# Maxima over partitions by two matmuls, x ahead of the weights, and a wider pace of phase one

## The chip, the core and the metric

The kernel runs on one core of a Trainium2 chip. A core has a matrix engine (TensorE, PE in the profile; PEld is its weight load), a vector engine (VectorE, DVE), an activation engine (ScalarE, ACT), a general engine (GpSimd, POOL) and a sync engine that issues most of the transfers (SyncE, SP). The engines share a 128-partition memory (SBUF), PE writes to banks of PSUM, and each engine takes its instructions strictly in its program's order. The metric is the device time of one execution in microseconds (us), and lower is better.

## The reference

Two branches work on x, 8192 rows of 448 values:

```
xn = layernorm(x)
s  = irfft2( soft( W2 . relu( W1 . rfft2(xn) + b1 ) + b2 ) )      # complex, 4 blocks of 112
g  = silu( ( gelu(xn @ w_gate) * (xn @ w_up) ) @ w_down )         # 448 -> 1792 -> 448
out = x + s * g
```

`soft` moves every value towards zero by 0.01 and cuts at zero. The transform runs over the 8192 rows. The result has to be FP32-accurate, so each FP32 value is split into two or three FP16 values, and a product becomes three FP16 matmuls. For the split, the weights are scaled by a power of two that is taken from the largest magnitude of a block.

## The kernel before

x is worked on in 16 chunks of 512 rows (each 4 tiles of 128 rows). Two streams of work share the engines.

The feed-forward stream (`ffn`, `chunk`, `unit`, `down`) goes over all chunks twice: pass 0 with the first 8 of 14 weight blocks of 128 columns, pass 1 with the other 6. That makes 32 feed-forward chunks, numbered 0 to 31 here. Each chunk first multiplies x by the gate and up weights (tiles `xta`, `xtb` by `wt`, into the banks `bx` and `by`), forms the gated product `h` on ACT, DVE and POOL, and then multiplies by the down weights (`h` by `dw`, into `bd`). Chunk 0 is special (`begin`, `token`, `plain`): it normalises and transposes its x itself, on PE, and starts while the weights are still being prepared.

The transform stream has three phases. Phase one (`chunk1`, once per x chunk) normalises x (`stats`, `norm`), makes the FP16 factors that the feed-forward stream reads later (stored to `xts` and read back transposed into `xta` and `xtb`), and does the first transform matmuls (`stage1`, `m` by `xs` into `bf`). Phase two (`zero`, then 32 groups in `group`) does the second transform stage, both complex layers and the way back. Phase three (`tiles3`) does the last inverse stage and writes the output.

The weights are prepared on the chip. `gu_block` finds the largest magnitude of one or two weight blocks: DVE reduces along the free dimension into `fm` and `fx`, and `largest` takes the maximum over the 128 partitions. From that come exponents (`fe`, `fh`, `fc`), and `gu_split` splits the block on ACT and DVE into `wt`. `gu_combs` loads the block again and forms sums and differences on POOL (`cb`), for a scheme that saves matmuls. `down_weights` does the same for the down weights (`dmx`, `dw`), `prep_mlp` for the weights of the transform's layers (`mst`, `ms`). `largest` is called 11 times: eight times for gate and up (five for chunk 0), twice for the down weights (once for chunk 0), once in `prep_mlp`. In the kernel before it is one POOL instruction, a collective over partitions:

```
G.partition_all_reduce(dst, src, channels=128, reduce_op=bass_isa.ReduceOp.max)
```

The order of the work is made by a small planner (`Pace`), not by hand. Every call of an engine goes through `Pace.issue` (so nearly all instructions carry line 167), which keeps a modelled clock for each engine with the costs in `Pace.cost`, and the coroutines of the kernel are continued in the order of these modelled times. The engines then run the instructions in that fixed order, each waiting on semaphores for what it needs. Two numbers set the pace of phase one: chunk c of phase one may start at the modelled time T1 + (c - 1) x DT. Phase two spreads its 32 groups evenly from its start to a fixed modelled time (END2, 1440), and phase three from there to END3 (1790). Memory for tiles is taken from rings with few buffers; four buffers (`wst`) hold raw weight blocks.

Of the kernel before, what the change touches and what calls it, by code (L numbers as in the profile page):

```python
# [22 lines left out]
CH = 4  # L23
# [12 lines left out]
EPS = 1e-5  # L36
# [8 lines left out]
class Pace:  # L45
# [96 lines left out]
    def cost(self, e, op, n, out, ins):  # L142
# [4 lines left out]
        if e == "ACT":  # L147
            return 0.17 + 0.00086 * n
        if e == "POOL":
            if op == "partition_all_reduce":  # L150
                return 4.0
            return 1.3 if n < 8 and op == "tensor_tensor_pow" else 0.2 + 0.0024 * n
        two = len([i for i in ins if i.free_size() == n and i.space != bass.MemoryType.PSUM]) > 1
        return 0.12 + (0.0014 if two else 0.00107) * n
# [136 lines left out]
def afno_geglu_kernel(ctx, tc, x, gu, wd, mlp, b1, b2, c_m, c_mt, c_small, out):  # L291
# [46 lines left out]
    fx = cp.tile([128, 2, NBK], F32, name="fx")  # L338
# [18 lines left out]
    def largest(dst, src):  # L357
        G.partition_all_reduce(dst, src, channels=128, reduce_op=bass_isa.ReduceOp.max)
# [17 lines left out]
    SX = ring(p1, [128, 4 * 480], F16, "sx", 2)  # L376
    YS = ring(p1, [128, 2, 2, D], F16, "ysb", 2)
# [16 lines left out]
    def load_x(c):  # L394
        x4 = EV["x4", c] = yield from X4.get()
        n2 = CH * (c % NG)
        for a in ((0, 2) if c == 0 else (0,)):
            m = 2 if c == 0 else CH
            Q.dma_start(x4[:, a:a + m, :], xv[:, n2 + a:n2 + a + m, :])
        if c == 0:  # L400
            Q.dma_start(ident, c_small[:, 0:128])
        yield
        done("xl", c)
# [7 lines left out]
    def stats(c, E, gap=True):  # L411

        x4 = EV["x4", c]
        st = yield from ST.get()
        s6, mv, rs = st[:, :, 0:6], st[:, :, 6:8], st[:, :, 8:12]
        for a in range(CH):
            V.bn_stats(s6[:, a, :], x4[:, a, :])
            V.bn_aggr(mv[:, a, :], s6[:, a, :])
            if gap:
                yield  # L420
        v, y, t, r = (rs[:, :, i] for i in range(4))
        E.tensor_scalar(v, mv[:, :, 1], EPS, None, op0=ALU.add)
        G.tensor_tensor(y, v, mhalf, op=ALU.pow)
# [5 lines left out]
        EV["st", c] = st  # L429
# [118 lines left out]
    def gu_block(b, to):  # L548
# [20 lines left out]
        V.tensor_scalar(mxa, mxa, 2.0 ** -30, None, op0=ALU.max)  # L569
# [4 lines left out]
        MX.put(mxa)  # L574
# [63 lines left out]
    def down_weights(p):  # L638
# [40 lines left out]
        largest(dmx[:, 14 + fp0:14 + fp0 + nf], dmx[:, fs])  # L679
        yield  # L680
# [884 lines left out]
```

## Time and profile before

| What | Value |
|---|---|
| median of 3 runs | 1992.36 us (1990.3 to 1993.31) |
| profiled execution | 1995.1 us, span 1993.3 us |
| PE busy in the span | 1827.8 us (92%), mean granted clock 0.976 |
| DVE, ACT, POOL busy | 1162.6 (58%), 976.5 (49%), 602.1 (30%) us |
| chain that ended last, by engine | PE 73%, DVE 6%, DMA 5%, issue 4%, POOL 4% |
| DMA | 288.10 MB, mean 145 GB/s |

The profile shows one execution. The tables by stretches give, for each stretch of the span in us, its length, the busy time and instruction count of each engine, the clock that PE was granted (1 is full), the share of time that the DMA engines were busy, and what they moved. In the timelines a row has its start and duration in us, engine, line, operation, output and inputs, shape, and a count of merged instructions; in brackets stands how long the engine had been idle before it, and what ended that. "issue" there means that nothing in the profile was waited for.

### The profile page before, as it was taken

The numbers are of one execution on the slowest core, as the hardware profiler recorded it, in microseconds if no ns is written. First come the engines' busy times: TensorE is split into PE (matmuls) and PEld (weight loads), VectorE is DVE, ScalarE is ACT, GpSimd is POOL, SyncE is SP. The second block draws the span as 40 slices with busy tenths as digits, with TensorE's granted clock in tenths as the row PEclk, the third lists the DMA queues.
The fourth block names the chain that finished last, engine by engine and source line by source line (L and its number), as shares of the span: only waits on it lengthen the run. The fifth ranks groups of instructions, "written<-read, shape, count | busy, mean of one in ns | idle before, by whom it ended". The sixth has DMA issues, their size and how long they took to land.

```text
span 1993.3 us, 36110 instructions
## 1 busy us (share of the span) xinstructions
PE 1827.8 (92%) x14665; PEld 1348.7 (68%) x14665; DVE 1162.6 (58%) x1777; ACT 976.5 (49%) x1675; POOL 602.1 (30%) x612
## 2 busy tenths in 40 slices
PE   0777798897899999999999999999999999999998
PEld 0336566565677678778778778777777677777666
DVE  3577487677676554455455445566665456555445
ACT  1356455555465456555456455555555333333333
POOL 0177365464354312122112112112121233332111
PEclk9988899999899999999999999999999999999999
DMA  3465664665556330422221354334342698877662
GB/s 135 144 197 149 177 198 143 199 207 166 170 168 174 90 103 11 109 61 71 66 82 45 113 172 111 87 97 108 85 108 71 199 335 272 275 228 215 173 179 91
DMA packets 326296, 288.10 MB, mean 145 GB/s; under 512 B 236560, under 2 KB 293520, under 8 KB 326128
## 3 DMA queue, kind: packets, MB, share of 16 engines
q1 hardware_dynamic: 325984, 285.06, 48.8%
q8 instruction: 115, 1.88, 0.4%
q10 hardware_dynamic: 144, 0.72, 0.1%
q14 instruction: 53, 0.43, 0.1%
HBM read 129.36 MB, written 105.58 MB: 118 GB/s over the span
## 4 chain that ended last, share of the span: by engine, by line
PE 73%; DVE 6%; DMA 5%; issue 4%; POOL 4%; ACT 2%; SPq 2%; POOLq 0%; DVEq 0%; ACTq 0%
PE bx L167 23%; PE bd L167 20%; PE by L167 16%; PE bf L167 14%; DMA xta<-xts 2%; SPq L167 2%; DMA pt<-prt 1%; DVE h L167 1%; POOL st L167 1%; POOL xs L167 1%; DMA mt<-c_mt 1%; POOL cb L167 1%; DVE x L167 1%; DVE u L167 1%; POOL v L167 0%
## 5 line engine op out<-in xcount | busy, mean ns | idle before, releaser
L167 PEld LDWEIGHTS <-wt 128*128 128x128 f16 x8622 | 848.1, 99 | 220.8 <-issue 66.9
L167 PE MATMUL bx<-xta,wt 128*128 128x256 f16 (+1 forms) x4086 | 522.9, 281 | 37.1 <-ACT u L167 25.7
L167 PE MATMUL bd<-dw,h 128*128 128x448 f16 x2688 | 536.7, 355 | 17.9 <-DVE dw L167 5.8
L167 PEld LDWEIGHTS <-h 128*128 128x128 f16 x2688 | 262.7, 98 | 258.7 <-issue 23.1
L167 PE MATMUL by<-xtb,wt 128*128 128x256 f16 x2160 | 264.9, 276 | 22.2 <-ACT u L167 22.2
L167 POOL TENSOR_TENSOR v<-v,u 128x512 f32<-128x512 f32 x108 | 147.7, 1368 | 432.9 <-ACT v L167 339.1
L167 ACT COPY v<-bx 128x512 f32<-128x512 f32 x216 | 126.1, 584 | 123.5 <-PE bx L167 122.7
L167 PE MATMUL by<-xta,wt 128*128 128x256 f16 x1296 | 161.1, 275 | 0.0
L167 DVE SCALAR_TENSOR_TENSOR gl<-v,fc,gl 128x512 f32<-128x512 f32 (+1 forms) x123 | 97.6, 803 | 106.0 <-ACT gl L167 86.0
L167 DVE TENSOR_TENSOR h<-u,h 128x512 f16<-128x512 f32 x116 | 117.6, 1014 | 55.0 <-ACT h L167 54.4
L167 POOL TENSOR_TENSOR o<-o,c 128x896 f32<-128x896 f32 (+2 forms) x33 | 69.3, 2099 | 249.6 <-DVE c L167 249.6
L167 PE MATMUL bx<-xtb,wt 128*128 128x256 f16 x1080 | 135.6, 273 | 0.1
L167 DVE TENSOR_TENSOR u<-by,u 128x512 f32<-128x512 f32 x108 | 74.2, 687 | 84.8 <-PE by L167 84.7
L167 POOL TENSOR_TENSOR o<-o,x 128x448 f32<-128x448 f32 x60 | 80.6, 1347 | 125.6 <-DVE o L167 107.6
L167 POOL TENSOR_TENSOR wn<-h,wn 112x512 f16<-112x512 f32 (+2 forms) x36 | 37.8, 1049 | 267.0 <-issue 190.5
L167 ACT ACTIVATE gl<-bx,fc 128x512 f32<-128x512 f32 (+1 forms) x123 | 76.4, 635 | 82.5 <-PE bx L167 81.9
L167 ACT ACTIVATE u<-u,fc 128x512 f32<-128x512 f32 (+1 forms) x123 | 80.5, 667 | 65.5 <-DVE u L167 65.3
L167 DVE SCALAR_TENSOR_TENSOR u<-v,fc,u 128x512 f32<-128x512 f32 (+1 forms) x123 | 102.0, 839 | 9.2 <-ACT u L167 3.2
L167 ACT COPY u<-by 128x512 f32<-128x512 f32 x108 | 63.1, 584 | 84.8 <-PE by L167 61.8
L167 PE MATMUL bf<-z,w1t 112*112 112x512 f16 (+2 forms) x432 | 96.8, 357 | 4.7 <-DVE z L167 4.3
L167 ACT COPY u<-bx 128x512 f32<-128x512 f32 x108 | 62.9, 583 | 72.8 <-PE bx L167 72.2
L167 DVE TENSOR_TENSOR h<-gl,h 128x512 f16<-128x512 f32 x108 | 82.3, 762 | 23.5 <-ACT h L167 23.2
(133 smaller groups left out, 2210.4 us busy)
## 6 DMA issues: line engine op xcount, KB each, us to landing
xts<-sx SPq DMA_DIRECT2D x32, 480.0 KB, 2.7
wst<-in_gu SPq DMA_DIRECT2D x21, 704.0 KB, 5.8
x<-in_x SPq DMA_DIRECT2D x32, 448.0 KB, 6.0
x<-in_x SPq DMA_DIRECT2D x16, 896.0 KB, 6.0
t<-ysb SPq DMA_DIRECT2D x64, 224.0 KB, 3.1
prt<-th SPq DMA_DIRECT2D x64, 224.0 KB, 2.0
pt<-prt SPq DMA_DIRECT2D x64, 224.0 KB, 3.3
u<-t SPq DMA_DIRECT2D x32, 448.0 KB, 4.7
```

Of the source, the lines that this page charges most:

```text
L167: return self.pace.issue(self.name, kind, out, ins, lambda: fn(out, *args, **kw))
```

## The change

Three things change, and the planner's costs with them.

`largest` leaves POOL. It now takes the maximum over partitions by two FP32 matmuls with an FP32 identity matrix (`identf`). The first has the data as its stationary operand and the identity as the moving one, so its output is the transposed data, with w columns of partition maxima now on w partitions and 128 values along the free dimension. DVE takes the maximum along these 128 values into a small tile (`mxr`). The second matmul has this value, repeated 128 times, as stationary operand, and the identity of size w as moving one: its output has the w maxima on all 128 partitions. DVE reads it from PSUM, with a floor of 2 to the -30 (or 0) applied in the same instruction.

The first chunk of x comes in four loads of one tile each, in the order 0, 2, 1, 3, all on SP and ahead of the first weight block, which moves from ACT's queue to SP's. The FP16 identity moves to ACT's queue. Chunk 0's statistics are taken in two halves, tiles 0 and 2 first, each with its own power on POOL. ACT's first table load for Gelu stands behind the issue of the loads.

Phase one's T1 goes from 68 to 72 and its DT from 31 to 40, so that its 16 chunks are planned over more of the feed-forward stream. The cost model gets other numbers for ACT, POOL and DVE; these have no part in the computation, but they move instructions everywhere.

```
-            return 0.17 + 0.00086 * n
+            return 0.19 + 0.00086 * n + (0.08 if op != "copy" and n > 128 else 0.0)
...
-    def largest(dst, src):
-        G.partition_all_reduce(dst, src, channels=128, reduce_op=bass_isa.ReduceOp.max)
+    def largest(dst, src, floor):
+
+        w = src.shape[-1]
+        b = yield from BF.get()
+        T.matmul(b[0:w, 0:128], src, identf, start=True, stop=True)
+        yield
+        r = yield from MX.get()
+        V.tensor_reduce(r[0:w, 0:1], b[0:w, 0:128], axis=AXIS.X, op=ALU.max)
+        yield
+        T.matmul(b[:, 128:128 + w], r[0:w].to_broadcast([w, 128]), identf[0:w, 0:w], start=True, stop=True)
+        MX.put(r)
+        yield
+        V.tensor_scalar(dst, b[:, 128:128 + w], floor, None, op0=ALU.max)
+        BF.put(b)
...
         if c == 0:
-            Q.dma_start(ident, c_small[:, 0:128])
+            S.dma_start(ident, c_small[:, 0:128])
+            for a in (0, 2, 1, 3):
+                Q.dma_start(x4[:, a, :], xv[:, n2 + a, :])
+                pace.then(lambda a=a: done("xl", 0, a))
+            return
...
-    T1, DT = 68.0, 31.0
+    T1, DT = 72.0, 40.0
...
-            (S if f == 0 and not again else Q).dma_start(t, gu[f])
+            Q.dma_start(t, gu[f])
...
-        mxa = yield from MX.get()
-        mc = yield from MX.get()
-        V.tensor_copy(mc, mx)
-        largest(mxa, mc)
-        MX.put(mc)
-        yield
+        yield
+        mxa = fx[:, :, NBK + b]
+        yield from largest(mxa, mx, 2.0 ** -30)
...
+        def half(q):
+            yield from stats(0, V, (q, q + 2))
+            for a in (q, q + 2):
                 norm(0, a)
-                tasks.append(pace.spawn(token(a, xs), pace.last))
+                tasks.append(pace.spawn(token(a, xss[a // 2]), pace.last))
                 yield
+
+        yield ev("xl", 0, 2)
+        V.tensor_copy(identf, ident)
+        yield from half(0)
+        yield from half(1)
```

Three places show how the instructions move. The first is POOL at the start of the program. Before (`mxa` is the maximum over partitions, `st` the statistics of chunk 0, `xs` its FP16 halves; an `ISA` row without operands prepares POOL for other instructions):

```order
L167 MEMSET mhalf 128x4
L167 ISA
L167 ISA mxa<-mxa 128x2
L167 ISA
L167 TENSOR_TENSOR st<-st,mhalf 128x4
L167 ISA
L167 ISA mxa<-mxa 128x2
L167 ISA
L167 TENSOR_TENSOR xs<-x_95,xs 128x448
```

and in the change:

```order
L172 MEMSET mhalf 128x4
L172 ISA
L172 TENSOR_TENSOR st<-st,mhalf 128x2
L172 TENSOR_TENSOR xs<-x_95,xs 128x448
L172 TENSOR_TENSOR st<-st,mhalf 128x2
L172 TENSOR_TENSOR xs<-x_95,xs 128x448
L172 TENSOR_TENSOR cb<-wst 128x256
```

The collectives and the `ISA` rows around them are gone, one `ISA` row is left ahead of the first power, and the power now comes twice, for two tiles each.

The second place is a maximum for a far weight block, in feed-forward chunk 3. Before, on POOL (`sf`, `sx` are factors of phase one, `v` a partial sum of the feed-forward stream):

```order
L167 TENSOR_TENSOR sf<-x_1951 128x256
L167 ISA
L167 ISA mxa<-mxa 128x2
L167 ISA
L167 TENSOR_TENSOR sf<-x_1951,sf 128x192
L167 TENSOR_TENSOR v_2603<-v_2603,u_2506 128x512
```

In the change it is on PE, amid the gate and up matmuls of that chunk; the second matmul of the pair follows 39 matmuls later, behind `by<-xta,wt_79`:

```order
L172 MATMUL by<-xtb,wt_77 128x256
L172 MATMUL bf<-identf,fx 2x128
L172 LDWEIGHTS wt_76
L172 MATMUL bx<-xta,wt_76 128x256
...
L172 MATMUL by<-xta,wt_79 128x256
L172 MATMUL bf<-identf,mxr 128x2
L172 LDWEIGHTS wt_76
L172 MATMUL bx<-xtb,wt_76 128x256
```

POOL has its factors and partial sums in a row now, and PE has two short matmuls more, the second of which needs DVE's reduction.

The third place is the start of phase two on SP: the load of `y` from the first transform stage. Before, the ninth transposed load `xta` stands ahead of it (for feed-forward chunk 9):

```order
L167 DMA xts<-xs 128x2x128
L167 DMA_TRANSPOSE xta<-xts 128x16x256
L167 DMA y<-t 128x896
L167 DMA_TRANSPOSE xtb<-xts 128x9x256
L167 DMA prt<-th 128x448 x4
```

In the change eleven of them do:

```order
L172 DMA xts<-xs 128x2x128
L172 DMA prt<-th 128x448
L172 DMA y<-t 128x896
L172 DMA_TRANSPOSE xta<-xts 128x16x256
L172 DMA_TRANSPOSE xtb<-xts 128x9x256
```

Phase two starts in feed-forward chunk 11 instead of chunk 8, and in both orders ends in chunk 22. In chunks 1 to 6 stand 108 matmuls of `stage1` instead of 135.

More of the change, by code (lines that the diff above doesn't have):

```diff
@@ L409, in load_m, with stats @@
         done("m", c)
[L411 removed]
+    def stats(c, E, tiles=range(CH)):
         x4 = EV["x4", c]
[L414 removed]
+        if ("st", c) not in EV:
+            EV["st", c] = yield from ST.get()
+        st = EV["st", c]
         s6, mv, rs = st[:, :, 0:6], st[:, :, 6:8], st[:, :, 8:12]
[L416 removed]
+        for a in tiles:
+            if c == 0:
+                yield ev("xl", 0, a)
             V.bn_stats(s6[:, a, :], x4[:, a, :])
             V.bn_aggr(mv[:, a, :], s6[:, a, :])
[L419 removed]
+            if c:
                 yield
[L421 to L423 removed]
+        sl = slice(tiles[0], tiles[-1] + 1, tiles[1] - tiles[0])
+        v, y, t, r = (rs[:, sl, i] for i in range(4))
+        E.tensor_scalar(v, mv[:, sl, 1], EPS, None, op0=ALU.add)
+        G.tensor_tensor(y, v, mhalf[:, 0:len(tiles)], op=ALU.pow)
         yield
@@ L754, in prep_mlp @@
         m = ms[:, 2:6]
-        largest(m, st)
-        yield
+        yield from largest(m, st, 0.0)
         e1, e2, eH, eO = (ms[:, i:i + 1] for i in (6, 7, 8, 9))
```

41 lines of the change are left out of this document (19 added, 22 removed).

## The prediction

> **What bounds the kernel now.** I read the stages first: the busy time of each engine in seven stretches that I cut at the ends of the feed-forward chunks (150.42 below is the first matmul of chunk 1; chunk 7 is 576.8 to 634.4).
>
> ```profile
> core 0: us, PE busy (x) PEld busy (x) DVE busy (x) ACT busy (x) POOL busy (x), PEclk, DMA share, GB/s
> 0.00:50.00 50.00, 4.41 (x24) 2.19 (x24) 18.16 (x49) 7.37 (x15) 4.81 (x11) 1.00 0.35 134
> 50.00:148.90 98.90, 74.71 (x327) 34.81 (x328) 67.02 (x120) 44.26 (x75) 43.67 (x64) 0.88 0.55 171
> 148.90:576.80 427.90, 363.01 (x2593) 260.85 (x2591) 301.84 (x504) 227.49 (x415) 215.87 (x277) 0.92 0.60 176
> 576.80:634.40 57.60, 57.17 (x434) 42.24 (x432) 44.50 (x70) 33.93 (x62) 29.78 (x38) 1.00 0.63 171
> 755.50:1572.00 816.50, 811.85 (x7343) 626.63 (x7341) 444.89 (x616) 449.58 (x735) 165.00 (x108) 1.00 0.32 89
> 1572.00:1993.30 421.30, 399.96 (x2980) 292.62 (x2978) 221.90 (x309) 152.86 (x259) 115.56 (x87) 0.99 0.75 225
> ```
>
> From 576.8 on PE is the bound: it is idle 0.4 us in chunk 7 and 4.7 in the 816.5 after 755.5. Before that it is not: 45.6 us idle in the first 50, and chunks 1 to 6 take 427.9 us. Chunk 7 has the same matmuls (24 of the transform per chunk, 135 in those six), so six such chunks would take 6 x 57.6 = 346 us: 82 us are lost, 64.9 as idle time (427.9 - 363.0) and 17 as slower matmuls (363 - 346; granted clock 0.92). So I asked what PE waits for, first in the head, on POOL's timeline.
>
> ```profile
> 10.46 0.37 POOL L167 PARTITION_ALL_REDUCE mxa<-mxa  x1 [9.64 <-DVE st L167]
> 19.88 1.06 POOL L167 TENSOR_TENSOR st<-st,mhalf 128x4 f32<-128x4 f32 x1 [9.05 <-issue]
> 26.89 0.73 POOL L167 PARTITION_ALL_REDUCE mxa<-mxa  x1 [5.95 <-issue]
> 34.55 1.02 POOL L167 TENSOR_TENSOR xs<-x,xs 128x448 f16<-128x448 f32 x1 [6.94 <-issue]
> 41.66 0.37 POOL L167 PARTITION_ALL_REDUCE mxa<-mxa  x1 [6.09 <-issue]
> 49.02 1.02 POOL L167 TENSOR_TENSOR xs<-x,xs 128x448 f16<-128x448 f32 x1 [7.00 <-issue]
> 51.84 7.21 PE L167 MATMUL bx<-xta,wt 128*128 128x256 f16 x44 [0.31 <-ACT xta L167]
> ```
>
> The collective itself is short (0.37). But each change between it and an ordinary instruction leaves POOL 5.95 to 9.05 us with nothing to wait for ("issue"), in both directions. The normalisation's power (19.88) and two halves of x (34.55, 49.02) are queued behind, and the first real matmul starts at 51.84. In chunks 1 to 6 the same pair stands at five places; here the second of them on the timeline of all engines, then PE's rows at the others.
>
> ```profile
> 306.24 0.37 POOL L167 PARTITION_ALL_REDUCE mxa<-mxa  x1 [6.81 <-DMA xts<-xs]
> 313.31 0.58 POOL L167 TENSOR_TENSOR sf<-x,sf 128x192 f32<-128x192 f32 x1 [6.70 <-issue]
> 313.92 0.35 ACT L167 CAST sx<-sf 128x192 f16<-128x192 f32 x1 [8.17 <-POOL sf L167]
> 314.81 1.44 PE L167 MATMUL bx<-xta,wt 128*128 128x256 f16 x6 [6.96 <-ACT u L167]
> ...
> 226.85 0.35 PE L167 MATMUL bf<-xs,m 128*128 128x448 f16 x1 [3.11 <-DVE ysb L167]
> 234.89 0.90 PE L167 MATMUL bf<-xs,m 128*128 128x448 f16 x2 [7.68 <-POOL xs L167]
> 397.54 2.29 PE L167 MATMUL by<-xtb,wt 128*128 128x256 f16 x10 [6.34 <-ACT u L167]
> 479.62 2.29 PE L167 MATMUL by<-xtb,wt 128*128 128x256 f16 x10 [7.00 <-ACT u L167]
> 544.01 2.29 PE L167 MATMUL by<-xtb,wt 128*128 128x256 f16 x10 [8.49 <-ACT u L167]
> ```
>
> PE names ACT, ACT's own row names POOL, and POOL waited for nothing: ACT's eviction copy stands behind a cast that needs POOL. That is how a 0.37 us operation on an engine busy 30% stops PE for 7.
>
> **The head, -28 us.** Removed are six collectives and the changes around them. The chain that is left runs through DVE, and the last thing chunk 0 needs of it is the last split of the down weights.
>
> ```profile
> 20.97:51.80 30.83, 5.84 (x32) 3.03 (x33) 12.03 (x31) 5.28 (x12) 3.14 (x4) 1.00 0.13 47
> 51.80:132.30 80.50, 56.71 (x238) 25.70 (x238) 58.05 (x105) 36.75 (x65) 33.81 (x45) 0.87 0.47 152
> 132.33 16.59 PE L167 MATMUL bd<-dw,h 128*128 128x448 f16 x80 [1.71 <-DVE dw L167]
> 150.42 1.47 PE L167 MATMUL bx<-xta,wt 128*128 128x256 f16 x12 [0.47 <-DMA xta<-xts]
> ```
>
> From the power's end (20.9) to that split (132.3) DVE works 70.1 of 111.3 us, 63%. In the changed order two statistics (0.8 each) and two reductions (1.2 each) come behind the power too: 74. One load of POOL's code is left ahead of the first power. Its price is not shown for that place; nearest is the 9.05 after the first collective, started at 0.8, so the power ends at 0.8 + 9.05 + 1.06 = 11 (below: x halves land earlier and nothing is loaded, about 7). The Trainium skill's page "GPSIMD Engine Reference", section Instruction dispatch, puts about 6 us on the first call of freshly loaded code; by it the power would end near 8 and the sum be 3 us better; POOL's rows here run from 5.95 to 9.05 and I stay with the nearest. At DVE 100% busy the last split ends at 11 + 74 = 85, at today's 63% at 129. I take 80%, in the middle: 104, 28 earlier than 132.3. Chunk 1 follows it by the same 18.1 us as now (150.42 - 132.3: the last 16.6 us of matmuls and the transposing load), since the load on SP stays behind the first partial sum's store. Bounds -47 and -3.
>
> ```profile
> 0.00:10.00 10.00, 0.00 (x0) 0.00 (x0) 3.09 (x8) 1.49 (x2) 0.29 (x5) 1.00 0.82 311
> 6.77 1.22 DVE L167 TENSOR_REDUCE fm<-wst 128x2 f32<-128x1024 f32 x1 [6.77 <-DMA wst<-in_gu]
> ```
>
> The first weight block now stands behind all of x, 0.9 MB, on SP's queue instead of beside it on ACT's: at 311 GB/s 3 us, so it lands near 10 instead of 6.8. The wait for the power, until 11, covers it, as it covers the earlier first half of x: nothing; with the power at 7 it would be the 3 us.
>
> **The five places in chunks 1 to 6, -50.** PE's idle rows: 7.68 + 6.96 + 6.34 + 7.00 + 8.49 + 3.11 = 39.6 us. The slow clock behind them is shared out by idle time: 17 x 39.6 / 64.9 = 10.4. Together 50.
>
> **The two matmuls in their place, +7.** No 128-column FP32 matmul is in the trace; the nearest is the one on the sums of absolute values.
>
> ```profile
> L167 PEld LDWEIGHTS bf<-ab,onesf x8: 188/190/192, 515.0 to 522.7; 112*128 112x128 f32 x8
> L167 PE MATMUL bf<-ab,onesf x8: 537/538/542, 515.1 to 523.1; 112*128 112x448 f32 x8
> ```
>
> Four calls gave eight rows, two passes each. With 128 of 448 columns a pass is 0.15 us beside a 0.19 load: 0.7 for the first matmul, some 0.5 for the second, 1.2 for a pair and 6 for the five on PE's path; in the head PE is idle anyway. Between the two PE may arrive before DVE's reduction; the order leaves it 10 to 40 matmuls of other work, so I add 1. Above: uncut passes (0.54 + 0.19, four to a pair) are 15 for five pairs. Below: nothing, if the loads overlap. The second change has a queue price: PE is in order, so what stands behind a waiting second matmul waits too.
>
> **The lower pace in chunks 1 to 6, -10.** What is left of the 82 is 32: the largest piece is POOL and DVE late for the transform of the next chunk.
>
> ```profile
> 184.51 0.53 PE L167 MATMUL bf<-xs,m 128*128 128x448 f16 x1 [7.32 <-ACT xs L167]
> 180.00:190.00 10.00, 3.43 (x14) 1.89 (x14) 8.39 (x10) 4.69 (x7) 9.04 (x12) 0.50 0.01 2
> ```
>
> By the order the six chunks now hold 108 transform matmuls instead of 135, a fifth less. But without the stalls the rest comes in less time: DVE's 302 us, less some 18 for the work moved out, over 427.9 - 76 = 352 is 81% instead of 71%; chunk 7 runs clean at 77% (44.5 of 57.6). So I give a third back. Bounds 0 and -32.
>
> **A denser second phase, +5.** The phase now starts two to three chunks later and ends at the same chunk (the 23rd): 12 chunks do what 14 did. Even with everything 1.2 times denser DVE goes from 54% (444.89 of 816.5) to 65%, below chunk 7's 77%. I double the idle time there, 4.7. Bounds 0 and +25, three chunks of today's mean loss in chunks 1 to 6 halved (82 / 6 = 14, 7 each, rounded up). The last 421 us hold the same chunks and the same third phase, and PE sets their pace: nothing.
>
> **Sum:** -28 - 50 + 7 - 10 + 5 = -76. The profiled run has a span of 1993.3 and a time of 1995.1, 1.8 around it; it becomes 1917 and 1919. It was 2.7 above the median of the three runs, 1992.36, which becomes 1916.
>
> **The rivals.** *DVE takes over.* It feeds every eviction; nearly 100% busy where POOL's data come late, it could give half of the head and of the five places back and all of the pace: -14 - 25 + 7 + 5 = -27, about 1965; a milder form, last split at 118 and 15 us lost again in the chunks, gives -14 - 35 + 7 + 5 = -37, 1955. For it: 81% on an engine in order. Against it: chunk 7. *The pace takes all the rest* and DVE runs full in the head: -47 - 50 - 32 + 2 = -127, 1865. Against it: the head needs ACT, DVE and PE in turn for each weight block. *The second phase cannot be squeezed* (slower than before).
>
> ```profile
> 739.52 0.88 PE L167 MATMUL bf<-sm,y 128*112 128x128 f16 x12 [1.07 <-DMA y<-t]
> 1572.37 12.44 DMA xta<-xts
> ```
>
> Its 32 groups run from 739.5 to about 1572, 26.0 us each, through single buffers. In the change I expect the first near 122 + 11 x 59 = 771 and the end at 1572 - 76 = 1496: 22.7 each. If the chain of a group has a floor at 26.0, the phase ends at 1603, 107 later, and the run takes 2023; it is slower than before from a floor of 22.7 + 76 / 32 = 25.1. Against it: PE's only idle time there is 4.7 us, so PE and not the chain sets today's 26.0. *The collective is not the cause* and the matmuls only add: POOL's code loads stay in some other form, 1992 + 7 = 1999 at most. The Trainium skill, "GPSIMD Engine Reference", Engine selection, assigns a reduction along partitions to GPSIMD; by that rule the change would be this case. POOL's rows around each collective speak against it: no run here shows that price without one.
>
> **How the numbers follow.** Forecast 0.57, DVE takes over 0.22, the pace takes all 0.14, no squeeze 0.04, not the cause 0.03. The single bounds would reach from 1862 (-47 - 50 - 32 and nothing added) to 1992 and beyond; 1872 to 1958 leaves out about half of the pace case and the worse half of the DVE case, under 2 in 10. About 0.2% (4 us) can be told from no change here: faster 0.93, same 0.03, slower 0.04.
>
> **What would show it.** Right: POOL without idle "issue" rows behind 12 us; the first matmul on xta at 23 to 32; chunk 1's first at 108 to 136; chunks 1 to 6 in 60 to 64 us each, with no PE idle row over 5; idle PE time under 15 us between chunk 11 and the third phase; FP32 matmul rows under 0.3 us. Wrong: rows of 6 us and more on POOL beside the power; DVE at 95% over whole chunks with PE waiting for h, ysb or u; PE waiting for z in the second phase; PE waiting at second matmuls for over 2 us each.

## The result, and the profile after

The changed kernel takes 1887.53 us (median; 1886.4 to 1892.75) where the kernel before takes 1992.84 (1990.3 to 1998.72): a ratio of 0.9473, 95% interval 0.9445 to 0.95. The forecast was 1916, in a range of 1872 to 1958; the direction and the range hold, and the gain is 105 us where the sum made it 76. The profiled execution has a span of 1884.7 us. Cut at the ends of the feed-forward chunks, as before (109.4 is the end of chunk 0, 475.3 of chunk 6, 1478.5 of chunk 22), its stages read:

```profile
core 0: us, PE busy (x) PEld busy (x) DVE busy (x) ACT busy (x) POOL busy (x), PEclk, DMA share, GB/s
0.00:50.00 50.00, 32.63 (x175) 17.30 (x176) 40.21 (x99) 22.90 (x45) 3.74 (x9) 1.00 0.61 211
50.00:109.40 59.40, 46.94 (x200) 20.30 (x200) 44.32 (x73) 28.76 (x44) 40.81 (x62) 0.89 0.70 220
109.40:475.30 365.90, 346.83 (x2586) 253.16 (x2586) 284.27 (x460) 210.72 (x384) 178.65 (x230) 0.99 0.61 181
475.30:530.30 55.00, 55.00 (x424) 41.30 (x423) 40.77 (x56) 31.48 (x58) 23.15 (x27) 1.00 0.54 151
696.70:1478.50 781.80, 776.84 (x7121) 598.62 (x7120) 444.35 (x632) 441.28 (x725) 168.31 (x112) 1.00 0.35 100
1478.50:1884.70 406.20, 390.27 (x2940) 287.69 (x2938) 220.97 (x304) 151.84 (x258) 112.44 (x85) 1.00 0.74 223
```

The first two rows are the head, which ends at 109.4 instead of 148.9; PE is busy 79.6 us of it, where it was busy 79.1 us of the longer one. The third row is chunks 1 to 6: 365.9 us instead of 427.9, idle time 19 instead of 65, and the granted clock 0.99 instead of 0.92. The 1003.2 us of chunks 7 to 22 are as long as before (1001.5). The rest, 406.2 us, holds the work of the 415.0 behind 1578.3 before, but for six matmuls of the third phase (0.24 us of PE each on average) that now stand in chunk 22. Taken from the end of one chunk to that of the next, the 108.6 us between the two spans come, but for 0.8 us behind the last chunk, as

| stage | before, us | after, us | difference | forecast |
|---|---|---|---|---|
| chunk 0 (the head) | 148.9 | 109.4 | -39.5 | -28 |
| chunks 1 to 6 | 427.9 | 365.9 | -62.0 | -50 + 7 - 10 = -53 |
| chunks 7 to 22 | 1001.5 | 1003.2 | +1.7 | +5 |
| chunks 23 to 31 | 408.3 | 400.3 | -8.0 | 0 |

In the head POOL no longer stands still between two pieces of work. Here are the rows of the timeline of all engines that answer to those of before:

```profile
5.73 0.72 POOL L172 TENSOR_TENSOR st<-st,mhalf 128x2 f32<-128x2 f32 x1 [4.91 <-DVE st L172]
9.51 1.22 DVE L172 TENSOR_REDUCE fm<-wst 128x2 f32<-128x1024 f32 x1 [1.71 <-DMA wst<-in_gu]
14.29 0.70 POOL L172 TENSOR_TENSOR st<-st,mhalf 128x2 f32<-128x2 f32 x1 [4.79 <-DVE fx L172]
21.57 3.64 PE L172 MATMUL bx<-xta,wt 128*128 128x256 f16 x22
92.79 16.60 PE L172 MATMUL bd<-dw,h 128*128 128x448 f16 x80 [1.51 <-DVE dw L172]
110.88 1.47 PE L172 MATMUL bx<-xta,wt 128*128 128x256 f16 x12 [1.50 <-DMA xta<-xts]
```

The first power waits for DVE's statistics and for nothing else, and starts at 5.73 where it started at 19.88. The first matmul on the transposed chunk comes at 21.57 instead of 51.84. The last split of the down weights releases PE at 92.79 instead of 132.33, and chunk 1 follows it by 18.1 us, exactly as before. Between the first power's end and that split, DVE hardly pauses now:

```profile
6.50:92.80 86.30, 62.98 (x295) 29.44 (x296) 77.30 (x155) 44.34 (x79) 33.87 (x46) 0.94 0.58 204
```

It works 77.3 of 86.3 us, 90%, where it worked 63% before. The maxima on PE cost this; the view groups one tile's instructions (shortest, median and longest duration in ns, first and last start):

```profile
L172 PEld LDWEIGHTS bf<-identf,mxr x22: 180/183/329, 15.6 to 440.0; 2*128 2x128 f32 x16, 8*128 8x128 f32 x2, 6*128 6x128 f32 x2, 4*128 4x128 f32 x2
L172 PE MATMUL bf<-identf,mxr x22: 246/267/369, 15.6 to 440.0; 2*128 2x2 f32 x16, 8*128 8x8 f32 x2, 6*128 6x6 f32 x2, 4*128 4x4 f32 x2
L172 PE MATMUL bf<-identf,fx x16: 272/273/417, 12.6 to 308.4; 128*2 128x128 f32 x16
L172 DVE TENSOR_REDUCE mxr<-bf x11: 268/269/280, 15.3 to 438.8; 2x1 f32<-2x128 f32 x8, 8x1 f32<-8x128 f32 x1, 6x1 f32<-6x128 f32 x1, 4x1 f32<-4x128 f32 x1
```

Eleven maxima gave 22 rows: each FP32 matmul is two passes, as the forecast said, but a pass takes 0.27 us and not 0.15. The two overlap, so the timeline shows them as 0.38 together:

```profile
244.32 0.38 PE L172 MATMUL bf<-identf,fx 128*2 128x128 f32 x2
249.25 0.38 PE L172 MATMUL bf<-identf,mxr 2*128 2x2 f32 x2
```

A maximum costs PE 0.8 us, and neither of these two rows has a wait before it: PE has other matmuls in the 4.9 us between them.

### The profile page after: what moved, and what is told of

The parts are those of the page before. It is cut to its first block, busy times and chain, and to the rows that moved or that the text cites. A ratio compares the mean times of both kernels' runs of the same rounds, so it can differ in the third digit from the quotient of the medians.

```text
span 1884.7 us, 36137 instructions
## 1 busy us (share of the span) xinstructions
PE 1814.3 (96%) x14709; PEld 1342.4 (71%) x14709; DVE 1186.5 (63%) x1787; ACT 975.7 (52%) x1675; POOL 591.4 (31%) x602
## 5 line engine op out<-in xcount | busy, mean ns | idle before, releaser
L172 PEld LDWEIGHTS <-wt 128*128 128x128 f16 x8622 | 839.0, 98 | 182.9 <-issue 25.3
L172 PE MATMUL bx<-xta,wt 128*128 128x256 f16 (+1 forms) x4086 | 511.6, 277 | 22.7 <-ACT u L172 13.5
L172 PE MATMUL by<-xtb,wt 128*128 128x256 f16 x2160 | 259.2, 273 | 1.2 <-ACT u L172 1.2
L172 DVE TENSOR_TENSOR h<-u,h 128x512 f16<-128x512 f32 x116 | 128.6, 1108 | 49.3 <-ACT h L172 48.9
L172 DVE SCALAR_TENSOR_TENSOR gl<-v,fc,gl 128x512 f32<-128x512 f32 (+1 forms) x123 | 96.6, 796 | 79.1 <-ACT gl L172 75.8
L172 ACT ACTIVATE th<-bd,fb 128x448 f32<-128x448 f32 x64 | 40.4, 633 | 122.9 <-PE bd L172 78.1
```

What stands on the lines that cost most here:

```text
L172: return self.pace.issue(self.name, kind, out, ins, lambda: fn(out, *args, **kw))
```

## The experiments

All times are medians, and ratios are against runs of the kernel before on the same chip. Where two kernels are compared, the difference is that of their ratios times 1993 us. The stages are cut from PE's rows as above, in one profiled execution each, and so they scatter: the changed kernel, c1, c2 and e1 have the same order on PE, DVE and ACT through chunk 0, which took 109.4, 109.6, 112.4 and 113.0 us. A difference of 3 us in one head shows nothing by itself.

| kernel | us | ratio to before (95%) | chunk 0 | 1 to 6 | 7 to 22 | 23 to 27 | 28 to 31 |
|---|---|---|---|---|---|---|---|
| before | 1992.84 | | 148.9 | 427.9 | 1001.5 | 229.3 | 179.0 |
| after | 1887.53 | 0.9473 (0.9445 to 0.95) | 109.4 | 365.9 | 1003.2 | 223.0 | 177.3 |
| a1: after, collective back | 1933.5 | 0.9693 (0.9673 to 0.9713) | 131.6 | 397.5 | 998.1 | 227.5 | 168.8 |
| a2: after, old pace | 1914.69 | 0.9593 (0.9574 to 0.9612) | 117.5 | 408.1 | 995.0 | 220.4 | 168.5 |
| a3: after, old x loads | 1878.88 | 0.9418 (0.9404 to 0.9432) | 109.8 | 360.9 | 1001.8 | 229.3 | 169.4 |
| b1: before, maxima on PE | 1901.91 | 0.953 (0.9511 to 0.955) | 113.9 | 378.7 | 997.3 | 227.4 | 176.3 |
| b2: before, lower pace | 1957.52 | 0.9813 (0.9794 to 0.9831) | 148.2 | 407.9 | 999.0 | 224.4 | 170.2 |
| b3: before, both of these | 1890.27 | 0.9475 (0.9452 to 0.9498) | 110.8 | 374.1 | 1006.9 | 221.4 | 169.7 |
| c1: after, an unread collective | 1919.85 | 0.9624 (0.9606 to 0.9642) | 109.6 | 400.0 | 1001.7 | 227.8 | 174.5 |
| c2: after, two unread | 1910.99 | 0.9578 (0.956 to 0.9596) | 112.4 | 393.9 | 1001.8 | 218.9 | 175.6 |
| d1: a3, pace 44 | 1868.22 | 0.9362 (0.9346 to 0.9378) | 111.0 | 358.5 | 1000.5 | 220.8 | 169.5 |
| d3: a3, pace 50 | 1873.6 | 0.9389 (0.9373 to 0.9404) | 109.7 | 355.6 | 935.9 | 268.7 | 192.5 |
| e1: after, pt loads on ACT | 1892.62 | 0.9485 (0.9471 to 0.95) | 113.0 | 367.3 | 1003.4 | 231.0 | 168.8 |
| f1: after, pace 44 | 1884.59 | 0.9439 (0.9421 to 0.9456) | 111.8 | 364.6 | 999.4 | 233.4 | 168.4 |

(In d3 the second phase ends in chunk 25, so its last three columns hold other work than those of the others. In the others a few matmuls of the third phase already stand in chunk 22: 21 in a2, 12 in c2, 6 in the changed kernel and e1.)

### a1, a2, a3: one part of the change undone

In a1 the eleven maxima go back to POOL (the planner counts 4 us for each, as before the change):

```
-        T.matmul(b[0:w, 0:128], src, identf, start=True, stop=True)
-        ... (reduction on DVE, second matmul)
+        V.tensor_copy(c[:, 0:w], src)
+        G.partition_all_reduce(m[:, 0:w], c[:, 0:w], channels=128, reduce_op=bass_isa.ReduceOp.max)
```

> The changed kernel with POOL's collective back in the eleven maxima; loads of x, pace and costs as changed. Theory 'code changes' (the idle time around the collective was the loss; the maxima by matmul are most of the gain of 105 us): 11 collectives bring back about 5 x 7 us of idle PE time plus slow clock in chunks 1 to 6 and 20 us or more in the head: 1945 to 1985 us, POOL rows with 6 us and more of 'issue' back. Rival 'pace' (the slower first phase is what emptied the stalls): 1900 to 1925.

In a2 the pace:

```
-    T1, DT = 72.0, 40.0
+    T1, DT = 68.0, 31.0
```

> The changed kernel with T1 and DT back at 68 and 31. 'Code changes': the pace is worth the 10 us of the forecast, 1893 to 1905, chunks 1 to 6 some 63 us each. Rival 'pace': 1920 to 1940, chunks 1 to 6 at 68 or more.

In a3 chunk 0's x comes in two loads again, with one statistic for all four tiles, and the first weight block goes back to ACT's queue. The FP16 identity goes first on SP's, and ACT's table load ahead of the loads (neither is in this cut):

```
-            for a in (0, 2, 1, 3):
-                Q.dma_start(x4[:, a, :], xv[:, n2 + a, :])
+        for a in ((0, 2) if c == 0 else (0,)):
+            m = 2 if c == 0 else CH
+            Q.dma_start(x4[:, a:a + m, :], xv[:, n2 + a:n2 + a + m, :])
...
-            Q.dma_start(t, gu[f])
+            (S if f == 0 and not again else Q).dma_start(t, gu[f])
```

> The changed kernel with x in two loads, the first weight block on ACT's queue, and chunk 0's statistics of all four tiles before one power. 'Code changes': the first power is released some 4 to 6 us later and the rest of the head follows: 1890 to 1897. Rival 'loads' (the early halves of x are what brought the head 39 us forward): 1905 to 1915.

Measured: a1 is 44 us slower than the changed kernel, 22.2 of them in the head and 31.6 in chunks 1 to 6. a2 is 24 slower; it loses 8.1 in the head and 42.2 in chunks 1 to 6, and has 19.6 of it back behind them. Both times, 1933.5 and 1914.7, lie between the ranges of the theory and of its rival: the maxima and the pace each matter, and neither range had the size. a3 is 11 us **faster**, where both of its ranges were slower: this set of changes to the first loads and statistics, called the x loads below, costs time. Its head ends where the other does (109.8 and 109.4), though its power is 5 us later, on a timeline of POOL and a window over all engines:

```profile
10.78 1.03 POOL L172 TENSOR_TENSOR st<-st,mhalf 128x4 f32<-128x4 f32 x1 [9.96 <-DVE fx L172]
11.90:94.30 82.40, 64.44 (x291) 29.96 (x292) 70.46 (x137) 42.23 (x74) 30.76 (x42) 0.90 0.54 182
```

POOL waits there for DVE, which has four statistics and a first maximum in front of the power, and not for its code. From 11.9 to the last split near 94, DVE is busy 86% with 70.5 us of work, against 90% with 77.3 us in the change. But in a3 more of DVE's work lies ahead of the power: counted from the first instruction, DVE works 76.5 of 94.3 us in a3 and 79.2 of 92.8 in the change. A power 5 us earlier brought the split forward by some 1.5 us, with 2.7 us more of DVE work ahead of it.

In a2 the order that the planner makes leaves PE behind POOL once for 12 us, and once at the first matmul of a pair, the queue price that the forecast named for the second:

```profile
252.10 0.59 PE L172 MATMUL bf<-identf,fx 128*2 128x128 f32 x2 [4.55 <-DVE fx L172]
451.99 0.20 POOL L172 MEMSET onesf<- 112x128 f32 x1 [18.43 <-DMA dsp<-wo]
454.81 0.90 PE L172 MATMUL bf<-xs,m 128*128 128x448 f16 x2 [12.13 <-POOL xs L172]
```

### b1, b2, b3: one part done alone

The same edits, made to the kernel before: b1 has the maxima on PE, with the old pace, loads and planner's costs; b2 has the lower pace alone; b3 has both.

```
-        G.partition_all_reduce(dst, src, channels=128, reduce_op=bass_isa.ReduceOp.max)
+        T.matmul(b[0:w, 0:128], src, identf, start=True, stop=True)
+        ...
-    T1, DT = 68.0, 31.0
+    T1, DT = 72.0, 40.0
```

> The kernel before with only the maxima by two matmuls (the FP16 identity loaded first on SP). 'Code changes': 1905 to 1920, the head's first gate matmul near 25 us, no PE idle row over 4 us in chunks 1 to 6. Rival 'pace': 1940 to 1960, because phase one at the old pace still crowds DVE and POOL.

> The kernel before with only T1 and DT at 72 and 40. Forecast of the prediction's term, alone: 10 us off, 1980 to 1990. Rival, from the run of the changed kernel at the old pace (27 us slower than the changed kernel): 1960 to 1970. If the pace mends only what the maxima by matmul leave behind: 1990 or more.

> The kernel before with the maxima by matmul and the new pace, old loads of x, old costs. If the parts add up as in the runs so far (maxima alone 94 us, pace 27): 1870 to 1880, as fast as the changed kernel with the old loads. If the pace helps only with the new costs: 1895 to 1902, as the maxima alone.

The maxima alone bring the ratio to 0.953, 94 us of 1993 (3 us beyond its range), with 35.0 us from the head and 49.2 from chunks 1 to 6. The pace alone brings 0.9813, 37 us, more than any of its three cases: 20.0 in chunks 1 to 6 and 13.7 in chunks 23 to 31. Together they are 0.9475, 105 us and not 131, between the two cases expected: once the stalls of the collective are gone, the pace brings 11 us more. From there to a3, whose only further difference is the planner's new costs, it goes to 0.9418, another 11; and from a3 to the change, which adds the x loads, 11 are given back. So the ladder from before to after is -94 - 11 - 11 + 11 = -105. (With the collective still in place the x loads and costs were worth much in the head: 131.6 in a1 against 148.2 in b2. They seem to win time that the maxima win anyway.)

### c1, c2: a collective that nobody reads

To measure the collective's price by itself: behind chunk 0's sites, at each of the five maxima in chunks 1 to 6, the changed kernel also runs POOL's collective on a scratch tile, whose result nobody waits for. c2 runs two of them, one straight behind the other.

```
+        NL[0] += 1
+        if NL[0] > 6:
+            G.partition_all_reduce(scr[:, 0:2], scr[:, 2:4], channels=128, reduce_op=bass_isa.ReduceOp.max)
```

> The changed kernel, and beside each of the five maxima after chunk 0 one POOL collective more on two columns of a scratch tile that nobody reads. Theory 'code changes': POOL stands still some 6 us ahead of it and 6 to 8 behind, PE loses 3 to 7 us at each place: 1900 to 1922 us. Rival 'waiting for the result' (in the kernel before, DVE and ACT were late because they waited for the maximum itself, not because POOL's other work was): nobody waits here, so 1886 to 1892.

> As the run before, with two unread collectives next to each other at each of the five places. Theory 'code changes': one change in and one out for both, so within 4 us of one collective. Rival 'the collective is slow itself': the loss is twice that of one.

c1 costs 30 us against the changed kernel, as the theory had it; its chunks 1 to 6 are 34.1 longer, near 7 a place. POOL's timeline at the first place of c1, and of c2:

```profile
166.07 1.19 POOL L174 TENSOR_TENSOR sf<-x 128x256 f32<-128x256 f32 x1
173.26 0.37 POOL L174 PARTITION_ALL_REDUCE scr<-scr  x1 [5.99 <-issue]
181.24 0.58 POOL L174 TENSOR_TENSOR sf<-x,sf 128x192 f32<-128x192 f32 x1 [7.61 <-issue]
```

```profile
168.84 1.06 POOL L174 TENSOR_TENSOR sf<-x 128x256 f32<-128x256 f32 x1
175.85 0.72 POOL L174 PARTITION_ALL_REDUCE scr<-scr  x2 [5.95 <-issue]
184.18 0.59 POOL L174 TENSOR_TENSOR sf<-x,sf 128x192 f32<-128x192 f32 x1 [7.61 <-DVE fe L174]
```

14 us of an engine for 0.37 us of work, and the second collective adds nothing but its own 0.35: what costs is the change from one kind of instruction to the other and back. For five of the twenty changes in c1 and c2 the profile names another engine in place of "issue" (here DVE's `fe`), but POOL's idle time there is as long as at the others. The other way round, "issue" alone does not show such a change. Behind chunk 9 the changed kernel has 27 waits of POOL of that name and no collective; most of them stand ahead of `wn` in the second phase (in the view of waits: us in total, times, longest):

```profile
POOL wn L172 <- issue: 123.5, 24, 14.5
```

The trace keeps the two apart by the instruction MODIFY_POOL_CONFIG (the `ISA` row without operands). It stands in a pair at each of the ten changes in c1, and in the changed kernel only once, at 0.76 us.

The way of the price to PE is the one read in the profile of before. The next three rows are from c1's timeline of all engines: ACT's cast waits for POOL, its eviction copy stands behind the cast, PE waits for the copy.

```profile
181.86 0.35 ACT L174 CAST sx<-sf 128x192 f16<-128x192 f32 x1 [8.51 <-POOL sf L174]
184.26 0.57 ACT L174 COPY u<-bx 128x512 f32<-128x512 f32 x1
184.89 2.72 PE L174 MATMUL bx<-xta,wt 128*128 128x256 f16 x12 [3.56 <-ACT u L174]
```

PE's window in c1's chunks 1 to 6 shows both halves of the price, 41 us idle and a clock of 0.95, against 19 and 0.99 in the changed kernel, with the same 2586 matmuls:

```profile
109.60:509.60 400.00, 359.18 (x2586) 258.49 (x2586) 279.18 (x455) 211.11 (x384) 181.77 (x228) 0.95 0.56 165
```

c2 is 9 us faster than c1 although it does more, where a difference within 4 was expected: in the profiled executions 6.1 in chunks 1 to 6 and 7.8 behind chunk 22, less 2.8 in the head. PE's order is the same in both up to 178 us and differs behind it. Where POOL's pause falls, and in which order the planner then puts the rest, seems to move a total by this much, and the 7 us a place of c1 hold such a share too.

### e1: the partial sums' loads on another queue

In the changed kernel the last chunks show a wait that chunks 28 to 31 of a3, with 169.4 us instead of 177.3, don't have. These are rows from the changed kernel's timeline; the number behind the start is the duration.

```profile
1697.47 3.90 SPq L172 DMA_TRANSPOSE xtb<-xts  x1
1703.05 0.38 SPq L172 DMA_DIRECT2D pt<-prt  x1
1704.88 0.68 DVE L172 SCALAR_TENSOR_TENSOR pt<-bd,fb,pt 128x448 f32<-128x448 f32 x1 [8.16 <-DMA pt<-prt]
1705.60 0.58 ACT L172 ACTIVATE th<-pt 128x448 f32<-128x448 f32 x1 [9.54 <-DVE pt L172]
1706.08 0.57 ACT L172 COPY u<-bx 128x512 f32<-128x512 f32 x1
1706.70 2.51 PE L172 MATMUL bx<-xta,wt 128*128 128x256 f16 x11 [2.54 <-ACT u L172]
```

The load of a stored partial sum is issued on SP behind a transposing load; DVE waits 8 us for it, ACT's tanh for DVE, the eviction copy behind the tanh, and PE for the copy. e1 issues these loads from ACT's queue:

```
-            Q.dma_start(t, prt[i][:, a * D:(a + 1) * D])
+            S.dma_start(t, prt[i][:, a * D:(a + 1) * D])
```

> The changed kernel, with one edit: the loads of the stored partial sums in the second pass of the feed-forward (pt<-prt, 64 of them) are issued from ACT's DMA queue instead of SP's, so that they no longer stand behind the transposing loads xta and xtb (8 and 4 us on SP's queue). Theory (the order on SP makes the slow form of the last chunks): chunks 28 to 31 take 169 to 171 us instead of 177.3, the two waits of 8 us and more of DVE for pt are gone, the rest of the run within 2 us: 1880, and most of the 9 us by which the old x loads were better is explained. Rival 1 (the x loads matter by themselves): chunks 28 to 31 get shorter, but chunks 1 to 4 keep the 6 us more than with the old x loads, so it stays 4 us or more above that run's 1878.9. Rival 2 (ACT is in order, and a load that waits for its buffer stops its evictions): PE waits for ACT's u in chunks 16 to 31, 1890 and more. Rival 3 (the late load is not what decides): chunks 28 to 31 stay at 177, 1887.

The two windows, of chunks 23 to 27 and 28 to 31, in the changed kernel and then in e1:

```profile
1478.50:1701.50 223.00, 219.81 (x1658) 161.81 (x1657) 125.69 (x172) 82.89 (x140) 74.71 (x57) 1.00 0.91 278
1701.50:1878.80 177.30, 170.47 (x1285) 125.88 (x1282) 92.45 (x128) 68.37 (x117) 37.73 (x28) 0.99 0.54 158
```

```profile
1483.70:1714.70 231.00, 222.90 (x1658) 162.97 (x1658) 128.41 (x175) 83.71 (x141) 75.80 (x59) 0.99 0.89 273
1714.70:1883.50 168.80, 168.32 (x1284) 125.27 (x1282) 91.27 (x127) 69.59 (x117) 38.17 (x28) 1.00 0.54 158
```

The last four chunks become fast (168.8). In the changed kernel PE waits there three times for ACT's u behind such a load, 2.54, 0.80 and 1.79 us of 6.8 us of idle time, and in e1 it does not. So the chain through SP's queue did stop PE. That it alone makes the 8 us is not shown: e1's edit moves the planner too, and from 1127 us on the order of the instructions is another. And chunks 23 to 27 lose the same 8, 5 as idle time and 3 as slower matmuls, and the head of this execution is 3.6 us longer at a lower clock (0.91 against 0.94) with the same instructions in the same order. The total is the same as the changed kernel's within the intervals, and not the 1880 of the theory. The wait was real, its removal worth nothing in all: in e1's chunks 23 to 27 PE has five waits of 1.2 to 3.2 us, for ACT's u, DVE's o and a transposing load, where the changed kernel has one.

### d1, f1, d3: a still lower pace

d1 and d3 are a3 with a pace of 44 and 50, f1 is the changed kernel with 44.

```
-    T1, DT = 72.0, 40.0
+    T1, DT = 72.0, 44.0      (d1, f1; d3: 72.0, 50.0)
```

> The kernel with the old x loads (1878.9 us) and a still lower pace of phase one: a chunk of the transform every 44 us of the planner's time instead of 40. By the order of the instructions chunks 1 to 6 hold fewer transform matmuls again, and the second phase begins one chunk later and ends at the same chunk, so that its 32 groups come in about 11 chunks instead of 12. Theory (what is left in chunks 1 to 6 is DVE and POOL being late, and the second phase has room): chunks 1 to 6 take 355 instead of 361, the matmuls moved out come back in chunks 7 to 22, and idle time falls by some 3 to 5 us in all: 1875. Rival 1 (nothing left to win): PE is busy throughout, the work only moves: 1878 to 1880. Rival 2 (the second phase cannot be squeezed further: a group's chain has a floor near the 24 us at which it runs now): PE waits for z or y in chunks 13 to 22 and it takes 1885 to 1900.

> The changed kernel with its four loads of x and the weight block behind them, and a pace of 44 us for a chunk of the transform instead of 40; it differs from the run with the old x loads and pace 44 (1868.2 us) in the loads and the statistics of chunk 0 alone. Theory (the x loads themselves are worth nothing; what they cost at pace 40 came from the order of instructions in which they happened to end, in chunks 1 to 4 and on the queue in the last chunks): 1866 to 1872, and the head ends within 2 us of that run's 111. Rival (the x loads cost their 9 us wherever they stand): 1875 to 1880, with chunks 1 to 6 some 6 us longer than that run's 358.5. A second rival (the pace of 44 helps only together with the old loads): 1885 to 1890.

> The kernel with the old x loads and a pace of 50 us. By the order of the instructions the second phase now lies in chunks 14 to 25 instead of 12 to 22, most of it in the shorter second-pass chunks, and the third phase in chunks 26 to 30 instead of 22 to 27, so that both have less room. Theory (PE is the bound nearly everywhere by now, and only idle time can be won): chunks 1 to 6 take 350 to 354 instead of 358.5, but the matmuls moved out come back later: 1863 to 1870, within 5 us of pace 44. Rival 1 (no room is left behind the second phase: the loads of the third phase come in fewer chunks and PE waits for them): PE idle 10 us and more in the chunks from 26 on, 1875 to 1890. Rival 2 (every step of the pace is worth the 10.7 us that 40 to 44 brought): 1852 or better.

d1 is the fastest kernel of all, 1868.22 us, 0.9362 of before: 11 us better than a3. Only 2.4 of that are in chunks 1 to 6; 8.5 are in chunks 23 to 27, where PE no longer waits at all. f1 has the same pace and is 15 us slower: its theory (1866 to 1872) missed, and the second rival (the pace of 44 helps only with the old loads, 1885 to 1890) comes nearest. Against the changed kernel f1 is 7 us faster, with intervals that overlap. Chunk 23 by itself is 58.0 us in f1 and 43.7 in d1, near 2 us of it for nine more matmuls of the third phase in f1; here are f1's, then d1's window over it:

```profile
1475.80:1533.80 58.00, 49.10 (x341) 34.21 (x341) 26.53 (x37) 16.57 (x28) 17.17 (x14) 0.88 1.01 323
```

```profile
1470.00:1513.70 43.70, 43.70 (x331) 32.21 (x330) 24.21 (x34) 16.78 (x28) 15.56 (x11) 1.00 0.97 316
```

The third phase begins there, and the DMA engines are full in both. In f1 its first matmuls stand on PE ahead of their data, as the timeline shows:

```profile
1475.07 0.46 SPq L172 DMA_DIRECT2D mt<-c_mt  x1
1480.76 1.27 PE L172 MATMUL bf<-u,mt 128*128 128x448 f16 x3 [4.95 <-DMA mt<-c_mt]
1486.55 0.68 DVE L172 SCALAR_TENSOR_TENSOR o<-bf,ms,g 128x448 f32<-128x448 f32 x1 [15.56 <-DMA g<-gsp]
```

Most of the rest of the difference is in chunks 1 to 6, 6.1 us (2.0 in chunk 1 and 3.3 in chunk 4). Between the changed kernel and a3 it is 5.0 there, 2.6 in chunk 1 and 3.3 in chunk 4. So the new x loads cost 5 to 6 us in chunks 1 and 4 at both paces. The order of the instructions is different in these chunks, though the code edited is chunk 0's; in chunk 4 PE waits for ACT's v and th, 1.2 to 2.5 us each, with the new loads, and 0.7 at most with the old. Which of the moved instructions makes these waits was not tried.

d3 is no faster than d1 (0.9389 against 0.9362) and just outside its theory's 5 us: chunks 1 to 6 take 2.9 us less than d1's, but the third phase has less room, and PE is idle 7.2 us from chunk 26 on, 5.6 of them in one wait for DVE's `pt` (its first rival had 10 and more).

```profile
1581.50:1862.40 280.90, 273.73 (x2029) 199.03 (x2028) 159.15 (x221) 101.65 (x171) 101.32 (x78) 0.99 0.93 298
1718.43 5.68 PE L172 MATMUL bd<-dw,h 128*128 128x448 f16 x18 [5.60 <-DVE pt L172]
```

## Why the prediction was right, and where it was not

**What bounds the kernel, and the collective as the cause: right.** c1 and a1 show it from both sides: the collective put back costs 44 us; put beside the matmuls of the five places and never read, 30. The rival "the collective is not the cause" is out, and with it, for this case, the Trainium skill's "GPSIMD Engine Reference", Engine selection, which gives a reduction along partitions to GPSIMD: for a [128, 2 to 8] tile two FP32 matmuls and a 0.27 us reduction on DVE do it for 0.8 us of PE.

**The head, -28 forecast, -39.5 measured.** The step was "11 + 74 us of DVE at 80%", the last split at 104. Three terms of it were off. The start: the first power ended at 6.45 (-4.5). The price of 9.05 was taken from a row behind a collective. Here MODIFY_POOL_CONFIG stands at 0.76, and whatever it cost was over within 4.9 us, behind the wait for DVE's statistics. The density, the largest: 90% instead of 80% (74 / 0.80 - 74 / 0.896 = -9.9). The work: 77.3 us instead of 74 (+3.7). Together 11 us, and the split came at 92.8. That the start decides little is a3's finding: its power ended at 11.8, later than the forecast's 11, and its head was as short, with DVE 86% busy behind the power and 70.5 us of work left. "18.1 us from the split to chunk 1" held to the tenth. Which part shortened the head is b1's: 35 of the 39.5 come from the maxima alone.

**The five places, -50, and the matmuls, +7: right in size.** In chunks 1 to 6 the maxima alone brought 49.2 (b1) where these two terms make 43. The pair costs 0.8 us, not 1.2, since the two passes overlap, and no pair in these chunks has a wait; so five are 4 us. The queue price showed only in other orders: 4.55 us in a2 and some 2 in d1, d3 and f1 at a pair's first matmul, and at the second, where the forecast had named it, 1.30 in d3 and once 3.15 in c2:

```profile
407.30 0.59 PE L174 MATMUL bf<-identf,mxr 6*128 6x6 f32 x2 [3.15 <-DVE mxr L174]
```

Undone from the other end (a1) the same step is worth 31.6. That the lower pace leaves more room for a late POOL would explain it, and was not tested.

**The lower pace, -10: the total was met by luck, its place was wrong.** Behind the maxima the pace is worth 11 us of the total (b1 to b3). But only 4.6 of those are in chunks 1 to 6, where the forecast put the whole term; 12.6 come behind chunk 22, 3.1 in the head, and 9.6 are given back in chunks 7 to 22. And the term is not one that can be added: it is 37 without the maxima, 11 with them, 24 with the new costs and loads as well (a2), as pace and costs go into one planner and change the whole order. (The working gives "a third back" of 32, which would leave 21; the term takes a third. And its 81% for DVE divides by 427.9 - 76, of which the 76 is not worked out; measured are 78%.)

**The denser second phase, +5: the size was near (+1.7), by luck.** The forecast doubled PE's idle time and moved no work into these chunks. Here are chunks 7 to 22, before and after:

```profile
576.80:1578.30 1001.50, 992.02 (x8780) 761.50 (x8778) 555.05 (x799) 545.13 (x912) 222.15 (x176) 1.00 0.35 97
475.30:1478.50 1003.20, 997.67 (x8813) 763.90 (x8812) 596.73 (x853) 561.47 (x945) 255.72 (x217) 1.00 0.39 108
```

PE's idle time fell from 9.5 to 5.5 us, and PE worked 5.7 us longer: 27 matmuls of the first phase and 6 of the third came in. (In the stretch whose 4.7 us the forecast doubled, it is 5.0 now.) The denser groups themselves came as forecast. Behind `zero` the 32 groups start at 757.4 (771 forecast) and run at 21.5 us a group (22.7 forecast; before, counted alike, 25.8). The rival with a floor at 25.1 fell by itself, and d1 goes further: 19.5 us a group, with PE idle 3 us in chunks 7 to 22.

```profile
757.42 0.83 PE L172 MATMUL bf<-sm,y 128*112 128x128 f16 x12
1422.55 0.84 PE L172 MATMUL bf<-sm,y 128*112 128x128 f16 x12
818.79 0.83 PE L172 MATMUL bf<-sm,y 128*112 128x128 f16 x12
1422.87 0.83 PE L172 MATMUL bf<-sm,y 128*112 128x128 f16 x12
```

(The first matmuls of the first and the last group, in the changed kernel and then in d1; 32 groups, so 31 steps between the two times.)

**The tail, 0 forecast, -8 measured.** "The same chunks, and PE sets their pace: nothing" was wrong. Of the 8 us, 4.6 are idle time and some 1.5 the six matmuls that moved to chunk 22; the rest goes with a clock of 1.00 instead of 0.99 in chunks 23 to 27. But for such matmuls (21 in a2, near 5 us), chunks 23 to 31 hold the same ones in all kernels but d3, and take 388.9 (a2) or 390.3 (d1) to 408.3 us (before). e1 and f1 show two places where it goes, a load behind a transposing load on SP and the first matmuls of the third phase ahead of their data; which of them an order has is not to be seen from the edit.

**The x loads, "nothing": wrong.** Nothing is right for the head: the weight block landed at 9.5, as worked out, and no more was lost than 1.7 us of DVE. For the kernel they cost 11 us by the ratios (a3), of which the two profiled executions show 7.6: 5.0 in chunks 1 to 6, 1.4 in 7 to 22 and 1.6 behind, less 0.4 in the head. At a pace of 44 they cost 15. The step left out that the edit changes the planner's order far behind the head. Which part of it does, the loads, the halves of the statistics, the identity or the table load, was not separated.

**What was to be seen.** "POOL without idle issue rows behind 12 us" held to chunk 9 and not as it was written: behind come the 27 waits of that name read under c1, 138 us in all, in a kernel without a collective, and before the change such waits stood there too (22 ahead of `wn`, 190.5 us). The sign was too wide, as the name of the wait is not that of its cause. No PE idle row in chunks 1 to 6 is over 5 (the longest is 3.6): right. PE's idle time from chunk 12's start to the third phase is 5 us, below 15. Chunk 1's first matmul at 110.88 is within 108 to 136; the first on the transposed chunk, 21.57, is earlier than 23. Chunks 1 to 6 take 67.7, 57.6, 59.0, 64.2, 55.3 and 62.1: the mean of 61 is within 60 to 64, most of them singly are not. FP32 rows have medians under 0.3.

**The rivals.** "DVE takes over" did not happen in the chunks (284.27 of 365.9 us, 78%, where it worked 71% before), and in the head a nearly full DVE was the gain and not the loss. The result, 1887.5, lies nearer to the 1865 of "the pace takes all the rest and DVE runs full in the head" (0.14) than to the forecast's 1916. In the head, -39.5 measured, that rival's -47 was nearer than -28; in chunks 1 to 6, -62 measured, it had -82 before what the matmuls cost, and the forecast's -53 was nearer. (The +2 in its sum is not worked out; the other rivals add 7 and 5.)

The shortfall of 32 us between the sum and the span (1917 and 1884.7) is then 11.5 in the head, 9 in chunks 1 to 6, 3 in the second phase and 8 in the tail.

## What to carry to other kernels

Look at an engine's idle time between two pieces of its own work, not at its share: a 0.37 us operation of another kind cost POOL 14 us of its queue and the kernel 6 to 7 of its time, even with a result that nobody read. Show the cause by adding the operation alone, since the name of a wait does not prove it. When a chain's head is taken away, the density of the engine that is left decides, and it can come near 90%; so work out how much of its idle time was a wait for what is removed. And where one planner orders all engines, each edit moves waits hundreds of microseconds away: terms overlap (94 and 37 made 105), and 10 us of a 400 us stretch can come or go by the order alone, so time each part both alone and undone.

## What the runs showed of the hardware that was not expected

- POOL pays for a change once, with two collectives behind it as with one, and the way back costs more. In c1 and c2 the ten changes to the collective took 5.88 to 6.80 us of idle time, those back to an ordinary instruction 6.83 to 8.79; two collectives in a row paid once. The Trainium skill's "GPSIMD Engine Reference", Instruction dispatch, gives about 6 us for the first call of freshly loaded code; the way there agrees, the way back is 1 to 3 us longer.
- At the start of the program no such price is seen: behind MODIFY_POOL_CONFIG at 0.76 the power started at 5.73, 0.15 us after DVE's last statistic (5.58). If anything was paid, it was over in 4.9 us, less than any change in c1 and c2 took.
- An FP32 matmul of 128 columns ran as two passes of 0.27 us that overlap to 0.38; a two-column one took as long (0.27 and 0.38).
- Idle time on PE went with a lower clock, and so cost twice: in c1 the same 2586 matmuls took 359.2 us of PE instead of 346.8, at a granted clock of 0.95 instead of 0.99.
